# A hand-planned order for attention and the first MoE matmuls: table loads charged, engines held for attention, first k and v in other tiles

## The chip, the cores and the metric

One Trainium2 chip, one core. The time is the device time of one execution in microseconds. TensorE (PE) multiplies, VectorE (DVE), ScalarE (ACT) and GpSimd (POOL) work element by element, and all loads are issued by the queue of SyncE (SP).

## What is computed

Packed attention, then two MoE layers, in fp32:

```python
p_packed = sm_attn(p, k, v)                    # 4 batches, 8 heads, 576 positions, 64 wide; 32 packed queries
out = sm_attn(q, p_packed, p_packed)           # softmax attention, twice
x = out.transpose(0, 2, 1, 3).reshape(2304, 512)
h = x @ w_in                                   # 512 x 2048
x = (h * sigmoid(1.702 * h)) @ w_out           # 2048 x 512
pn = probs / (probs.sum(-1) + 1e-9)            # 4 experts
out = sum over e of pn[:, e] * (relu(x @ w1[e]) @ w2[e])
```

`w_in` and `w_out` come as 64 bit floats and have to be brought to fp32 on the chip.

## The kernel before

**Units.** Attention is cut in 8 units (`units`, 4 batches of 2 groups of 4 heads). `pack(u)` does the first attention of a unit: four times three transposes of k on TensorE, each with a copy on ScalarE (`kT`), two scores, two maxima on VectorE, two exps on ScalarE, transposes of the exps with copies (`kv`, L371), a product with v, the division, a last transpose and the split in a high and a low part. `unpack(u)` does the second: transposes of q with copies (`qT`), two scores, a 32 by 32 transpose on VectorE, maximum, exp, sum, division on POOL, back transpose and the split `a`. In the text p3 is the pack and u3 the unpack of unit 3.

**Matmuls.** All large products are done in three passes of fp32r parts, high times high, low times high, high times low. `packed_w` multiplies the packed values with a quarter of `w_in` (`win`) and evicts `pw` (`packed_w_out`: ScalarE casts, VectorE subtracts); `l1_first` multiplies `pw` with `a` and evicts by two gelus (`l1_out`); `l2_first` multiplies with `wout` and adds to the `y` tiles (`l2_out`). `l2_first` needs all four `wout` of its part. One block is 288 tokens, half of a batch; the second layer of a block runs one block behind the first.

**Conversions.** `fetch_w` loads a 512 KB piece of `w_in` or `w_out`; `convert` brings it to fp32 and splits it: six VectorE instructions, one of POOL, a cast on ScalarE and a subtraction on POOL. Eight pieces are converted in the head for the first quarter, and up to four more (`MORE`) once six unpacks (`UNITS_DONE`) are done.

**Order.** The head stands in `manual_schedule`: engines execute in the order in which the program is written. That order is made by the class `Order`. Each activity is a generator that yields, before every step, the engine, the planned time in us and the PSUM banks it takes; `Order.run` keeps a planned time for each engine (`at`) and always lets the step go that can start first, and at the same start the one with the lower rank. Evictions (`packed_w_out`, `l1_out`, `l2_out`) have rank 1, the two lanes of attention (`LANES`) 2 and 3, conversions 4, the lane of MoE matmuls 9. The lanes run p0 p2 u0 u2 p4 p6 u4 u6 and p1 p3 u1 u3 p5 p7 u5 u7. `load(FIRST)` issues the first loads: k and v of units 0 to 3 (`load_kv`), q of 0 and 1, and eight pieces of weights. When both lanes and the conversions are done, the main loop goes on outside of `manual_schedule`: the rest of the first MoE (`moe_step`), then the second one, whose order the scheduler of the framework makes.

**Memory.** One pool of 29 slots (`big`) holds loads, operands and intermediate tiles; a tile waits for the readers of the tile that had its slot. The three `y` tiles of pool `yp` take the result of the first MoE, 12 KB in each partition.

**Probabilities.** `norm_probs` loads `domain_probs` into `pr` and divides by the sums. It stands behind the head in the program, outside of `manual_schedule`, and ran at its start. `pr` is read by `l2_second` (L741, L743) alone.

The functions that the change touches, and what calls them:

Of the kernel before, what the change touches and what calls it, by code (L numbers as in the profile page):

```python
# [8 lines left out]
F32 = mybir.dt.float32  # L9
# [10 lines left out]

LANES = ("p0 p2 u0 u2 p4 p6 u4 u6", "p1 p3 u1 u3 p5 p7 u5 u7")
FIRST = "k0 k1 F F F F k2 k3 q0 q1 F F F F"
HOP = 0.25
UNITS_DONE = 6
MORE = 4


class Order:

    def __init__(self, banks):
        self.free = banks
        self.at = {}
        self.parts = []
        self.on = False

    def add(self, part, rank, at=0.0):

        if not self.on:  # L40
            return self.drain(part)
        self.parts.append([rank, at, next(part, None), part])

# [8 lines left out]
    def run(self, while_):  # L52
        self.on = True
        while while_():
            best = None
            for p in self.parts:
                rank, at, ask, part = p
                if callable(ask):
                    t = ask()
                    if t is None:  # L60
                        continue
                    p[1] = max(at, t)
                    p[2] = self.send(p, p[1])
                    best = p
                    start = None
                    break
                engine, us, banks = ask
                if banks > self.free:
                    continue
                start = max(at, self.at.get(engine, 0.0))  # L70
                if best is None or (start, rank) < best[0]:
                    best, start_ = ((start, rank), p), start
            if start is None:
                continue
            assert best is not None, [p[2] for p in self.parts]
            (start, _), p = best
            engine, us, banks = p[2]
            self.free -= banks
            self.at[engine] = start + us
            p[1] = start + us + HOP  # L80
            p[2] = self.send(p, p[1])
        self.on = False
# [15 lines left out]
def packed_attention_moe_kernel(  # L98
# [33 lines left out]
    big = ctx.enter_context(tc.tile_pool(name="big", bufs=29))  # L132
    small = ctx.enter_context(tc.tile_pool(name="small", bufs=2))
    hp = ctx.enter_context(tc.tile_pool(name="hp", bufs=4))
# [62 lines left out]
    def convert():  # L197
# [12 lines left out]
        f32 = man.bitcast(F32)  # L210
        yield "DVE", 0.83, 0

# [6 lines left out]
        )  # L219
        yield "DVE", 1.2, 0  # L220
        nc.vector.tensor_scalar(
# [25 lines left out]
    def load_kv(u):  # L247

        b, g = units[u]
        h0 = G * g  # L250
        sl = [slot([SP, 3 * R * D], F32, f"kv{u}{i}") for i in range(3)]
        m = 2 * R * D
        raws["k", u] = []
        for j in range(2):
            kk = sl[j][:, :m].rearrange("p (r h d) -> p r h d", r=R, h=2)
            for h in range(2):
                nc.sync.dma_start(out=kk[:, :, h, :], in_=k[b, h0 + 2 * j + h].rearrange("(p r) d -> p r d", r=R))
            raws["k", u].append(sl[j][:, :m])
        for j in range(2):
            vv = sl[j][:, m:].rearrange("p (r d) -> p r d", r=R)  # L260
            nc.sync.dma_start(out=vv, in_=v[b, h0 + j].rearrange("(p r) d -> p r d", r=R))
        vv = sl[2][:, :m].rearrange("p (h r d) -> p h r d", r=R, h=2)
        nc.sync.dma_start(out=vv, in_=v[b, h0 + 2:h0 + 4].rearrange("h (p r) d -> p h r d", r=R))
        arrives(("k", u), 1.18)
        raws["v", u] = [sl[0][:, m:], sl[1][:, m:], sl[2][:, :R * D], sl[2][:, R * D:m]]

# [12 lines left out]
    def transposed_scores(pair, dst, scores):  # L279

        for s in range(2):
            for j in range(2):
                yield "PE", 0.4, 1
                ps = psum("ps_t")
                for r in range(3):
                    nc.tensor.transpose(ps[:, r * SP:(r + 1) * SP], pair[j][3 * s + r], ident[:SP, :SP])
                t = yield "ACT", 0.4, 0
                nc.scalar.copy(out=dst[:, j, s * HS:(s + 1) * HS], in_=ps[:, :HS])
                order.free += 1
        for s in range(2):  # L290
            yield "PE", 0.6, 1
            yield from scores(s)
# [39 lines left out]
    def pack(u):  # L332
        b, g = units[u]
        kr, vr = raws.pop(("k", u)), raws.pop(("v", u))
        st = small.tile([128, 8], F32, tag="st", bufs=4, name=f"st{u}")
        kT = slot([128, 2, S], F32, f"kT{u}")
# [13 lines left out]
        for s in range(2):  # L350
            yield "ACT", 0.7, 0
            nc.scalar.activation(
                out=E[:, s * HS:(s + 1) * HS], in_=pss[s][:, :HS], func=AF.Exp,
                bias=st[:, 2:3], scale=scale, accum_out=st[:, 4 + s:5 + s],
            )
            order.free += 1
# [6 lines left out]
        for s in range(2):  # L363
            yield "PE", 0.45, 1
            ps = psum("ps_e")
# [6 lines left out]
            order.free += 1  # L372
        yield "PE", 1.0, 1
        ps = psum("ps_v")
# [40 lines left out]
    def unpack(u):  # L415
# [17 lines left out]
        nc.vector.tensor_sub(out=t, in0=t, in1=s2[:, 0, :].unsqueeze(2).to_broadcast([128, NB, NP]))  # L433
        yield "ACT", 0.7, 0
        nc.scalar.activation(out=t, in_=t, func=AF.Exp, scale=scale)
# [23 lines left out]
    def packed_w(a, bp):  # L459

        for g in range(UG):
# [11 lines left out]
            for b in (2 * bp, 2 * bp + 1):  # L473
                PW[a, b, g] = slot([128, 2, 512], F32R, f"pw{g}")
            order.add(packed_w_out(a, bp, g, pss), 1, clock())

# [16 lines left out]
    def l1_first(a, j, c):  # L493
# [16 lines left out]
        h = hid[a, j, c // 2][:, 2 * (c % 2):2 * (c % 2) + 2, :]  # L510
        order.add(l1_out(h, ps), 1, clock())

    def l1_out(h, ps):
        yield "ACT", 0.82, 0
        g32 = gp.tile([128, HS], F32, tag="g", name="g32")
# [6 lines left out]
    def l2_first(a, j, t):  # L522
# [21 lines left out]
        order.add(l2_out(a, j, t, ps), 1, clock())  # L544

# [210 lines left out]
    def norm_probs():  # L756
        nc.sync.dma_start(out=pr, in_=probs.rearrange("(t p) e -> p t e", p=128))
        nc.vector.reduce_sum(out=prs, in_=pr, axis=AX.X)
        nc.vector.tensor_scalar_add(prs, prs, 1e-9)
        nc.vector.reciprocal(out=prs, in_=prs)  # L760
        nc.vector.tensor_mul(out=pr, in0=pr, in1=prs.unsqueeze(2).to_broadcast([128, NT // 128, NE]))
# [112 lines left out]
    with tc.manual_schedule(engines=engines):  # L874
# [5 lines left out]
        all_p()  # L880
        load(FIRST)
        order.on = True
        lanes = [lane(x) for x in LANES] + [conversions(2 * CPP, MORE)]
        for i, x in enumerate(lanes):
            order.add(x, 2 + i)
        order.add(moe_lane(), 9)
        order.run(lambda: any(p[3] in lanes for p in order.parts))
        for p in list(order.parts):
            order.finish(p)
    norm_probs()  # L890
    b_parts = {i: b_operand(i) for i in range(NPAIR)}
# [63 lines left out]
```

## Time and profile before

| | us |
|---|---|
| median of 3 runs | 1252.76 |
| lowest, highest | 1251.65, 1253.18 |
| profiled execution | 1249.63 |
| its span, first to last instruction | 1247.4 |
| TensorE busy in the span | 1175.7 |
| VectorE busy | 899.5 |
| ScalarE busy | 523.6 |
| POOL busy | 483.0 |

Times in the rows below count from the first instruction. A row of the timeline is one instruction or several of the same kind in a row (x6): start, length, engine, line of the program, operation, what it writes and reads; in brackets the idle time of the engine ahead of it and what ended that. Matmuls overlap, so a busy TensorE is not one at its peak. An fp32 product counts as two instructions, a transpose or an fp32r product as one. The granted clock is 1.00 at 2.4 GHz and 0.50 at 1.2 GHz; a window shows its mean.

### The profile page before, as it was taken

The page shows a single profiled execution, that of the slowest core. Times are in us where ns is not written, and L with a number is a line of the kernel's source. Part 1 is how long each engine was busy: PE and PEld are TensorE (multiplying, and loading weights), DVE is VectorE, ACT ScalarE, POOL GpSimd, SP SyncE. Part 2 cuts the span into 40 slices and gives each one's busy share as a digit, 9 for nine tenths or more (in the row PEclk, how much of TensorE's full clock was granted, in tenths as well). Part 3 has the DMA queues.
Part 4 walks back from the last instruction along what each step waited for, and adds up shares of the span by engine and source line. Part 5 has one row for each costly group of instructions (what it writes and reads, how often), then busy time and mean ns, then how long its engine had stood idle before and what let it go on. Part 6 is the DMA issues. An engine that isn't in the chain of part 4 may idle for free. (4 is left out here: it accounts for less than half of the span.)

```text
span 1247.4 us, 18269 instructions
## 1 busy us (share of the span) xinstructions
PE 1175.7 (94%) x6912; PEld 1062.0 (85%) x6912; DVE 899.5 (72%) x1652; ACT 523.6 (42%) x1152; POOL 483.0 (39%) x409
## 2 busy tenths in 40 slices
PE   5778788999999989999999989999999999999998
PEld 4467577999999989999999969999999789999997
DVE  4873678786875856777777876777778767777775
ACT  3567655444434634433333444333333353333321
POOL 1320023221120345544444664444444744444430
PEclk8779989999999989999999989999999899999999
DMA  8623321121110012222222132222221332222201
GB/s 234 177 76 82 85 66 54 51 69 52 51 35 18 1 51 69 68 68 69 68 68 68 34 118 69 68 68 68 68 69 41 95 119 68 68 68 68 68 18 51
DMA packets 90392, 87.46 MB, mean 70 GB/s; under 512 B 43968, under 2 KB 71616, under 8 KB 90304
## 3 DMA queue, kind: packets, MB, share of 16 engines
q1 hardware_dynamic: 90304, 86.30, 23.1%
q8 instruction: 54, 0.88, 0.3%
q14 instruction: 34, 0.28, 0.1%
HBM read 81.56 MB, written 4.72 MB: 69 GB/s over the span
## 5 line engine op out<-in xcount | busy, mean ns | idle before, releaser
L732 PE MATMUL ps_o<-w,h 128*128 128x512 f32 x1728 | 449.9, 396 | 9.7 <-ACT h L688 5.5
L680 PE MATMUL ps_p<-b,w 128*128 128x384 f32 x2016 | 402.8, 339 | 0.6 <-DVE o L743 0.6
L680 PEld LDWEIGHTS ps_p<-b,w 128*128 128x128 f32 x2016 | 362.8, 189 | 24.6 <-DVE o L743 0.9
L732 PEld LDWEIGHTS ps_o<-w,h 128*128 128x128 f32 x1728 | 323.4, 189 | 63.6 <-DVE h L689 7.2
L154 POOL TENSOR_TENSOR w<-raw,w 128x512 fp32r<-128x512 f32 x192 | 236.4, 1250 | 172.3 <-ACT w L153 170.5
L528 PE MATMUL ps_acc<-h,wout 128*128 128x288 f32 x1536 | 232.9, 300 | 6.1 <-DVE h L520 6.1
L528 PEld LDWEIGHTS ps_acc<-h,wout 128*128 128x128 f32 x1536 | 215.1, 191 | 10.0 <-DVE h L520 7.3
L743 DVE SCALAR_TENSOR_TENSOR o<-ps_o,pr,o 128x512 f32<-128x512 f32 x270 | 200.0, 741 | 5.1 <-PE ps_o L732 5.1
L154 POOL TENSOR_TENSOR w<-s,w 128x512 fp32r<-128x512 f32 x96 | 132.6, 1381 | 170.4 <-ACT w L153 170.4
L500 PE MATMUL ps_h<-a,pw 128*128 128x288 f32 x768 | 129.9, 305 | 19.1 <-ACT a L446 12.6
L153 ACT CAST w<-raw 128x512 fp32r<-128x512 f32 x192 | 106.9, 562 | 72.4 <-POOL w L154 48.0
L500 PEld LDWEIGHTS ps_h<-a,pw 128*128 128x128 f32 x768 | 113.6, 195 | 22.9 <-ACT a L446 13.4
L520 DVE TENSOR_TENSOR h<-g,h 128x288 fp32r<-128x288 f32 x128 | 73.4, 575 | 63.0 <-ACT g L517 62.0
L649 DVE TENSOR_TENSOR s<-raw 128x256 f32<-128x256 f32 x48 | 48.5, 1010 | 86.1 <-DMA raw<-in_moe_w_dram 69.8
L516 ACT ACTIVATE h<-ps_h 128x288 fp32r<-128x288 f32 x128 | 53.1, 415 | 96.5 <-PE ps_h L500 95.9
L688 ACT ACTIVATE h<-uv 128x384 fp32r<-128x384 f32 x48 | 25.2, 526 | 162.5 <-DVE uv L720 162.5
L706 DVE TENSOR_TENSOR u<-ps_p,p 128x384 f32<-128x384 f32 x48 | 26.7, 556 | 70.4 <-ACT p L702 67.2
L153 ACT CAST w<-s 128x512 fp32r<-128x512 f32 x96 | 59.1, 615 | 41.9 <-DVE s L650 19.2
L217 POOL TENSOR_SCALAR cvt<-cvt 128x512 uint32<-128x512 uint32 x32 | 23.9, 747 | 127.0 <-DVE cvt L214 108.4
L688 ACT ACTIVATE h<-c 128x384 fp32r<-128x384 f32 x48 | 25.2, 525 | 92.5 <-DVE c L714 92.5
L688 ACT ACTIVATE h<-p 128x384 fp32r<-128x384 f32 x48 | 25.2, 526 | 82.4 <-DVE p L720 82.4
L553 DVE TENSOR_TENSOR y<-ps_acc,y 128x288 f32<-128x288 f32 (+2 forms) x120 | 44.7, 388 | 11.2 <-PE ps_acc L528 11.0
(102 smaller groups left out, 1169.5 us busy)
## 6 DMA issues: line engine op xcount, KB each, us to landing
raw<-in_moe_w_dram SPq DMA_DIRECT2D x96, 512.0 KB, 3.9
raw<-in_moe_w_in_dram SPq DMA_DIRECT2D x16, 512.0 KB, 4.1
raw<-in_moe_w_out_dram SPq DMA_DIRECT2D x16, 512.0 KB, 3.8
kv<-in_k_dram SPq DMA_DIRECT2D x32, 144.0 KB, 3.3
q<-in_q_dram SPq DMA_DIRECT2D x32, 144.0 KB, 2.9
out_dram<-o SPq DMA_DIRECT2D x18, 256.0 KB, 2.0
kv<-in_v_dram SPq DMA_DIRECT2D x16, 144.0 KB, 3.0
kv<-in_v_dram SPq DMA_DIRECT2D x8, 288.0 KB, 3.5
```

Source lines behind the costliest of these rows:

```text
L153: nc.scalar.copy(out=hi, in_=src)
L154: eng.tensor_sub(out=lo, in0=src, in1=hi.bitcast(F32))
L500: nc.tensor.matmul(out=ps[:, :HS], lhsT=PW[a, b, g][:, wp, c * 128:(c + 1) * 128], rhs=A[b * UG + g][:, xp, s * HS:(s + 1) * HS], start=(m ...
L516: nc.scalar.activation(out=h[:, 0, :], in_=ps[:, :HS], func=AF.Gelu_apprx_sigmoid)
L520: nc.vector.tensor_sub(out=h[:, 1, :], in0=g32, in1=h[:, 0, :].bitcast(F32))
L528: nc.tensor.matmul(out=ps[:, :HS], lhsT=W["out", a, c][:, wp, t * 128:(t + 1) * 128], rhs=hid[a, j, c // 2][:, 2 * (c % 2) + hq, :], start ...
L553: nc.vector.tensor_add(out=dst, in0=src, in1=dst)
L649: nc.vector.tensor_add(out=s1, in0=Am["A21"], in1=Am["A22"])
L680: nc.tensor.matmul(out=ps, lhsT=Wop[n, a, wp, kk], rhs=Bop[i, b, xp, kk], start=(m == 0), stop=(m == 5),)
L688: nc.scalar.activation(out=h[:, 0, :], in_=src, func=AF.Relu)
L732: nc.tensor.matmul(out=ps, lhsT=h[:, c, hq, o:o + 128], rhs=W2[n, c][:, wp, :], start=(c == 0 and m == 0), stop=(c == 1 and m == 2),)
L743: nc.vector.scalar_tensor_tensor(out=acc, in0=ps, scalar=pr[:, tok, e:e + 1], in1=acc, op0=ALU.mult, op1=ALU.add,)
```

## The change

- `Order.run` chooses the step with the smallest sum of planned start, `late` and a handicap. `late` is 1.28 (`TABLE`) for a ScalarE step that needs another function table than the one that the plan had last, and it also counts in the step's planned end. Lanes and evictions have handicap 0, the lane of MoE matmuls 0.3, conversions 0.6. At equal sums the one earlier in the list goes: lanes stand ahead of evictions. An engine may so be left idle in the plan for a step with a smaller handicap that can start a little later.
- The exps of `pack` and `unpack` name the table "exp", `l1_out` names "gelu".
- Planned times are longer: two of the three conversion steps on VectorE (0.83 to 0.9, 1.2 to 1.5), transposes (0.4 to 0.5), scores (0.6 to 0.9), the transposes of the exps (0.45 to 0.7) and the product with v (1.0 to 1.5) on TensorE.
- k and v of units 0, 1 and 2 (`EARLY`) are loaded into `y` tiles, not into nine slots of `big`.
- Pool `small` has 4 buffers, not 2.
- The load of `pr` is issued behind `load(FIRST)`, and `norm_probs` is the last thing in `manual_schedule`.

```diff
+EARLY = (0, 1, 2)
+TABLE = 1.28
-    def add(self, part, rank, at=0.0):
+    def add(self, part, handicap, at=0.0):
...
-            for p in self.parts:
-                rank, at, ask, part = p
-                if callable(ask):
-                    t = ask()
+            for p in list(self.parts):
+                while callable(p[2]):
+                    t = p[2]()
                     if t is None:
-                        continue
-                    p[1] = max(at, t)
+                        break
+                    p[1] = max(p[1], t)
                     p[2] = self.send(p, p[1])
-                    best = p
-                    start = None
-                    break
-                engine, us, banks = ask
+                if p not in self.parts or callable(p[2]):
+                    continue
+                engine, us, banks, table = (p[2] + (None,))[:4]
                 if banks > self.free:
                     continue
-                start = max(at, self.at.get(engine, 0.0))
-                if best is None or (start, rank) < best[0]:
-                    best, start_ = ((start, rank), p), start
+                start = max(p[1], self.at.get(engine, 0.0))
+                late = TABLE if table not in (None, self.table) else 0.0
+                if best is None or start + late + p[0] < best[0]:
+                    best = start + late + p[0], start + late + us, p
...
-    small = ctx.enter_context(tc.tile_pool(name="small", bufs=2))
+    small = ctx.enter_context(tc.tile_pool(name="small", bufs=4))
...
-        sl = [slot([SP, 3 * R * D], F32, f"kv{u}{i}") for i in range(3)]
+        n = R * D
+        if u in EARLY:
+            t = yp.tile([128, KD, 2 * TB], F32, tag="y", name=f"kv{u}").rearrange("p k t -> p (k t)")
+            sl = [t[:SP, x * 3 * n:(x + 1) * 3 * n] for x in range(2)] + [t[:SP, 6 * n:8 * n]]
+        else:
+            sl = [slot([SP, 3 * n], F32, f"kv{u}{i}") for i in range(3)]
...
-            yield "ACT", 0.7, 0
+            yield "ACT", 0.7, 0, "exp"
...
-        yield "ACT", 0.82, 0
+        yield "ACT", 0.82, 0, "gelu"
...
     def norm_probs():
-        nc.sync.dma_start(out=pr, in_=probs.rearrange("(t p) e -> p t e", p=128))
...
         load(FIRST)
+        nc.sync.dma_start(out=pr, in_=probs.rearrange("(t p) e -> p t e", p=128))
...
-        for i, x in enumerate(lanes):
-            order.add(x, 2 + i)
-        order.add(moe_lane(), 9)
+        for x in lanes[:-1]:
+            order.add(x, 0.0)
+        order.add(lanes[-1], 0.6)
+        order.add(moe_lane(), 0.3)
         order.run(lambda: any(p[3] in lanes for p in order.parts))
         for p in list(order.parts):
             order.finish(p)
-    norm_probs()
+        norm_probs()
```

## Rows read from the trace of the kernel before

**Rows 1.** Windows: stretch, its length, busy us (count) by engine, clock, DMA share, GB/s.

```profile
17.00:50.00 33.00, 25.87 (x293) 16.85 (x291) 27.96 (x61) 16.82 (x54) 14.91 (x19) 0.69 0.89 246
50.00:76.00 26.00, 12.43 (x56) 7.66 (x56) 24.91 (x40) 12.66 (x25) 7.37 (x7) 0.63 0.35 91
76.00:122.00 46.00, 43.86 (x390) 37.77 (x391) 19.91 (x46) 36.54 (x88) 3.52 (x6) 0.95 0.32 78
122.00:138.00 16.00, 10.89 (x154) 6.82 (x153) 5.92 (x15) 10.54 (x30) 0.74 (x3) 0.89 0.24 55
138.00:161.00 23.00, 12.56 (x89) 10.35 (x88) 18.33 (x33) 15.18 (x32) 3.92 (x5) 0.88 0.28 83
250.00:1247.00 997.00, 978.17 (x5322) 896.86 (x5321) 730.50 (x1325) 381.48 (x804) 427.07 (x341) 0.99 0.20 62
```

**Rows 2.** Waits of TensorE, whole span: who waited for whom, us, times, longest.

```profile
PE ps_s L297 <- DVE cvt L213: 8.1, 1, 8.1
PE ps_h L500 <- ACT pw L482: 5.0, 2, 4.6
PE ps_t L286 <- DMA kv<-in_k_dram: 2.6, 2, 1.6
```

**Rows 3.** Timeline of TensorE: start, length, what, and the wait ahead.

```profile
55.99 0.73 PE L297 MATMUL ps_s<-qT,pT 128*64 128x288 f32 x2 [1.63 <-ACT qT L288]
...
74.63 1.77 PE L500 MATMUL ps_h<-a,pw 128*128 128x288 f32 x5 [2.81 <-ACT a L446]
...
81.87 1.02 PE L528 MATMUL ps_acc<-h,wout 128*128 128x288 f32 x6
...
160.74 1.57 PE L500 MATMUL ps_h<-a,pw 128*128 128x288 f32 x5 [8.62 <-ACT a L446]
```

**Rows 4.** Timeline of ScalarE, in 50:76.

```profile
64.75 0.62 ACT L235 CAST wout<-cvt 128x512 fp32r<-128x512 f32 x1 [5.99 <-DVE cvt L231]
```

**Rows 5.** Timeline of SP and VectorE, start; then a load's size and landing time.

```profile
1.24 0.57 SPq L757 DMA_DIRECT2D pr<-in_moe_domain_probs_dram  x1
1.85 3.97 SPq L257 DMA_DIRECT2D kv<-in_k_dram  x4
...
5.18 0.22 DVE L758 TENSOR_REDUCE prs<-pr 128x18 f32<-128x72 f32 x1
...
pr<-in_moe_domain_probs_dram SPq DMA_DIRECT2D x1, 36.0 KB, 3.6
```

**Rows 6.** Timeline of VectorE and POOL, in 58:74.

```profile
58.08 2.85 DVE L486 TENSOR_TENSOR pw<-ps_w,pw 64x512 fp32r<-64x512 f32 x4
...
64.59 0.48 DVE L425 STREAM_TRANSPOSE t<-ps_s 128x288 f32<-128x288 f32 x1
...
70.10 1.16 POOL L441 TENSOR_TENSOR t<-t,s 128x576 f32<-128x576 f32 x1 [0.54 <-DMA kv<-in_k_dram]
...
73.05 0.77 DVE L443 STREAM_TRANSPOSE t<-t 128x576 f32<-128x576 f32 x1
```

**Rows 7.** Conversions: window of tile cvt (VectorE, ScalarE, POOL); last step on POOL.

```profile
17.00:76.00 59.00, 32.25 (x48) 4.94 (x8) 15.36 (x16) 0.66 0.65 178
...
73.86 1.27 POOL L237 TENSOR_TENSOR wout<-cvt,wout 128x512 fp32r<-128x512 f32 x1 [2.60 <-ACT wout L235]
```

**Rows 8.** Timeline of TensorE and ScalarE: p6 from 121.9, then q of u5 and u6.

```profile
121.94 0.49 PE L368 MATMUL ps_e<-ident,kT 128*96 128x128 f32 x3
...
121.93 1.28 ACT L516 ACT_TABLE_LOAD   x1
123.22 0.41 ACT L516 ACTIVATE h<-ps_h 128x288 fp32r<-128x288 f32 x1
...
124.44 0.52 ACT L371 COPY kv<-ps_e 96x384 f32<-96x384 f32 x1
...
142.14 0.41 PE L286 MATMUL ps_t<-ident,q 96*128 96x96 f32 x3
...
145.95 0.39 ACT L288 COPY qT<-ps_t 128x288 f32<-128x288 f32 x1
```

More of the change, by code (lines that the diff above doesn't have):

```diff
@@ L36, in __init__ @@
         self.on = False
-    def add(self, part, rank, at=0.0):
+        self.table = None
+    def add(self, part, handicap, at=0.0):
         if not self.on:
             return self.drain(part)
-        self.parts.append([rank, at, next(part, None), part])
+        self.parts.append([handicap, at, next(part, None), part])
     def drain(self, part):
@@ L55, in run @@
             best = None
-            for p in self.parts:
-                rank, at, ask, part = p
-                if callable(ask):
-                    t = ask()
+            for p in list(self.parts):
+                while callable(p[2]):
+                    t = p[2]()
                     if t is None:
-                        continue
-                    p[1] = max(at, t)
+                        break
+                    p[1] = max(p[1], t)
                     p[2] = self.send(p, p[1])
-                    best = p
-                    start = None
-                    break
-                engine, us, banks = ask
+                if p not in self.parts or callable(p[2]):
+                    continue
+                engine, us, banks, table = (p[2] + (None,))[:4]
                 if banks > self.free:
                     continue
-                start = max(at, self.at.get(engine, 0.0))
-                if best is None or (start, rank) < best[0]:
-                    best, start_ = ((start, rank), p), start
-            if start is None:
-                continue
+                start = max(p[1], self.at.get(engine, 0.0))
+                late = TABLE if table not in (None, self.table) else 0.0
+                if best is None or start + late + p[0] < best[0]:
+                    best = start + late + p[0], start + late + us, p
             assert best is not None, [p[2] for p in self.parts]
-            (start, _), p = best
-            engine, us, banks = p[2]
+            _, end, p = best
+            engine, us, banks, table = (p[2] + (None,))[:4]
             self.free -= banks
-            self.at[engine] = start + us
-            p[1] = start + us + HOP
+            self.at[engine] = end
+            self.table = table or self.table
+            p[1] = end + HOP
             p[2] = self.send(p, p[1])
@@ L210, in convert @@
         f32 = man.bitcast(F32)
-        yield "DVE", 0.83, 0
+        yield "DVE", 0.9, 0
         nc.vector.tensor_scalar(out=ex, in0=hi, scalar1=0x7FF00000, scalar2=None, op0=ALU.bitwise_and)
@@ L219, in convert @@
         )
-        yield "DVE", 1.2, 0
+        yield "DVE", 1.5, 0
         nc.vector.tensor_scalar(
@@ L264, in load_kv @@
         arrives(("k", u), 1.18)
-        raws["v", u] = [sl[0][:, m:], sl[1][:, m:], sl[2][:, :R * D], sl[2][:, R * D:m]]
+        raws["v", u] = [sl[0][:, m:], sl[1][:, m:], sl[2][:, :n], sl[2][:, n:m]]
     def load_q(u):
@@ L282, in transposed_scores @@
             for j in range(2):
-                yield "PE", 0.4, 1
+                yield "PE", 0.5, 1
                 ps = psum("ps_t")
@@ L290, in transposed_scores @@
         for s in range(2):
-            yield "PE", 0.6, 1
+            yield "PE", 0.9, 1
             yield from scores(s)
@@ L334, in pack @@
         kr, vr = raws.pop(("k", u)), raws.pop(("v", u))
-        st = small.tile([128, 8], F32, tag="st", bufs=4, name=f"st{u}")
+        st = small.tile([128, 8], F32, tag="st", name=f"st{u}")
         kT = slot([128, 2, S], F32, f"kT{u}")
@@ L363, in pack @@
         for s in range(2):
-            yield "PE", 0.45, 1
+            yield "PE", 0.7, 1
             ps = psum("ps_e")
@@ L372, in pack @@
             order.free += 1
-        yield "PE", 1.0, 1
+        yield "PE", 1.5, 1
         ps = psum("ps_v")
@@ L433, in unpack @@
         nc.vector.tensor_sub(out=t, in0=t, in1=s2[:, 0, :].unsqueeze(2).to_broadcast([128, NB, NP]))
-        yield "ACT", 0.7, 0
+        yield "ACT", 0.7, 0, "exp"
         nc.scalar.activation(out=t, in_=t, func=AF.Exp, scale=scale)
@@ L474, in packed_w @@
                 PW[a, b, g] = slot([128, 2, 512], F32R, f"pw{g}")
-            order.add(packed_w_out(a, bp, g, pss), 1, clock())
+            order.add(packed_w_out(a, bp, g, pss), 0.0, clock())
     def packed_w_out(a, bp, g, pss):
@@ L510, in l1_first @@
         h = hid[a, j, c // 2][:, 2 * (c % 2):2 * (c % 2) + 2, :]
-        order.add(l1_out(h, ps), 1, clock())
+        order.add(l1_out(h, ps), 0.0, clock())
     def l1_out(h, ps):
-        yield "ACT", 0.82, 0
+        yield "ACT", 0.82, 0, "gelu"
         g32 = gp.tile([128, HS], F32, tag="g", name="g32")
@@ L543, in l2_first @@
                     ACC[i] = yp.tile([128, KD, 2 * TB], F32, tag="y", name=f"y{i}")
-        order.add(l2_out(a, j, t, ps), 1, clock())
+        order.add(l2_out(a, j, t, ps), 0.0, clock())
     def l2_out(a, j, t, ps):
```

## Prediction

> **What bounds the kernel now.** I read the windows by stage first [rows 1]. From 250 us to the end TensorE is busy 978 of 997 us: that is matmul work which the change doesn't touch. Before it, in the head (attention, with the first MoE work in its gaps), TensorE idles 13.6 of 26 us in 50:76 and 15.5 of 39 in 122:161, but only 2.1 of 46 in 76:122. TensorE is full afterwards, so a microsecond of matmul work that moves forward into a hole comes off the end; that is all the change can be worth.
>
> The waits of TensorE and its timeline name the holes. *Hole A* is 8.1 us up to the scores of u2 [rows 2] and 2.8 us up to 74.63, where the first `l1_first` gets `a` of u1; the second layer begins at 81.87 [rows 3]. ScalarE's queue shows one reason: the cast of a `wout` stood 6.0 us at its head, waiting for a VectorE conversion [rows 4], and in that order the `qT` copies that u2's scores need stood behind it. VectorE is what ended last: busy 24.9 of 26 us there and 28.0 of 33 in the stretch before [rows 1]. *Hole B*: the matmuls of batches 0 and 1 run out before attention delivers p7 and u5; the longest piece is the 8.6 us up to 160.74, for `a` of u5 [rows 3]. A *third hole*, 4.6 us for `pw` [rows 2], lies in the main loop.
>
> **The change part by part.** The sum is made against the profiled execution (1249.63 us, span 1247.4); the median of the runs shown is 1252.76, 3.13 more, and that is added at the end.
>
> *Probabilities.* The load of `pr` goes from ahead of the first k to behind FIRST; it takes 0.57 us of the SP queue, and the first k, now issued at 1.85, can go at about 1.28 [rows 5]. The start waits for loads, so I take 0.6. Bounds: 0, and the 3.6 us that this load needs to land [rows 5], if it holds up the others that long. Four small VectorE instructions (the first takes 0.22 [rows 5], so 0.9 together) move to the end of the head, after which `pr` is not read before the second MoE. Beside VectorE's other work they cost nothing; without cover 0.9.
>
> *First k and v in the y tiles, small pool of 4.* Nothing is computed otherwise; nine `big` slots are free sooner and loads that wait for slots can go earlier. TensorE waits for k loads only at the start, 2.6 us in two pieces [rows 2], when slots are not short yet. So 0; bounds 0 and 2.6. The y tiles are wanted at 81.87, when the packs of u0 to u2 are long done: no new wait.
>
> *Order in hole A.* The path is u1. Its second score ended at 56.72 [rows 3]; VectorE transposed it at 64.59, 7.9 us late, after `pw` evictions (2.85 for the second four) and steps of u0 [rows 6]. Its back transpose could go when POOL ended at 71.26 and went at 73.05, 1.8 late, behind conversion steps [rows 6]. Together 9.7. In the new order a lane step goes before an eviction that could start at the same time, and a conversion step starts only if no lane step is due within 0.6. Steps of 1.4 us that already run still have to end, and u0's own stay: I take half, 4.8. The new planned times, 3.76 us a conversion for 3.39, are nearer to the 32.25 us that VectorE took for eight, 4.03 each [rows 7], so casts should be queued less early. l1 then goes on at 69.8 rather than 74.63, and the second layer at 77.1 rather than 81.87. The next thing late would be the last `wout`, done at 75.13 [rows 7]: it just fits. Gain 4.8; far bound the two waits, 10.9; near bound a loss, the first rival.
>
> *Order in hole B.* After the exps of a pack ScalarE now changes to gelu, runs two of them, and only then copies what TensorE transposed. In p6 the first transposes end at 122.43 and the copy starts at 124.44, 2.0 late, with the table load and the gelus between [rows 8]; p4 and p5 show the same pattern. With 1.28 charged to the gelu the copy is due first. Lane 1 ends last and has one such pack, p5: 2.0. Then u5 and u6: q transposed by 142.55 were copied at 145.95, 3.4 late, behind gelu and `pw` casts [rows 8]; lanes now go first, I take 3.0. The granted clock in 138:161 is 0.88 [rows 1], part of it at the lower level after the wait; at full clock the 12.56 us of matmuls would be 1.5 shorter; I take 1.0. Sum 6.0; bounds 0 and 15.5, all idle of 122:161.
>
> *The charge against its price.* From the table load at 121.93 to the gelu is 1.29 us [rows 8], so 1.28 is right here. The Trainium skill (ScalarE: Activation LUTs, What ACT_TABLE_LOAD costs) gives 2.66 us for a switch, the load and a drain of 1.38 behind it. By that the plan would stay 1.38 short at every switch and the gain would come out as in the third rival. The rows show no such drain.
>
> *Waits that the change adds.* The 0.3 of the MoE lane makes the plan hold TensorE before a matmul chunk if a lane step is due so soon. Between 76 and 162 there are 76 lane steps on TensorE (4 packs of 10, 6 unpacks of 6), one each 1.1 us, so a chunk meets one with a chance of 0.27 and then waits 0.15 on the mean; 66 chunks (22 pairs of one l1 and two halves of an l2) give 2.7 us. Queued behind are matmuls, whose readers have slack. Part of it falls into time that is idle anyway: I take 1.3; bounds 0 and 2.7. The 0.6 of the conversions belongs to the first rival.
>
> *Main loop.* Its third hole depends on when conversions of the next part of `w_in` and `w_out` end against TensorE; both move with the head. Taken as unchanged; bounds 4.6 either way.
>
> Sum: 0.6 + 4.8 + 6.0 - 1.3 = 10.1 us. An execution like the profiled one then takes 1239.5, the median 1242.7.
>
> **The rivals.**
> *VectorE waits for attention and conversions come late (slower).* In 17:76 VectorE idles only 6.1 us [rows 1]. The plan may add up to 0.6 before each of 32 lane steps (4 packs of 5, 2 unpacks of 6), 19.2 at most, and the second layer needs all four `wout`. It decides from 6.7 us of added idle on: 75.13 + 6.7 is the 81.87 of now. At half the ceiling the second layer is 2.9 late, at all of it 12.5. For it: VectorE is the bound there. Against it: the plan waits only where a conversion is ready and a lane step near. With 4 us late, hole B moved along with it, and 0.6 gained at the start: 1256.2.
>
> *The gaps only change place (no change).* Attention comes earlier, but the MoE work that it passes comes later, and TensorE is 95% busy in 76:122 [rows 1]. For it: the plan now overstates TensorE at full clock (0.5 for three transposes that took 0.41 [rows 8]), so its order is off the other way. The 10.1 is lost again: 1252.8.
>
> *ScalarE still runs late against the plan (half the gain).* The exp is charged too, so gelus pass it, 0.7 us a pair by [rows 8], and copies of evictions with them; hole B then gives 1.5, not 6. 0.6 + 4.8 + 1.5 - 1.3 = 5.6: 1247.2.
>
> *Both holes close.* 10.9 of A and all but 3 of B's 15.5: 0.6 + 10.9 + 12.5 - 1.3 = 22.7: 1230.1.
>
> **How the numbers follow.** Forecast 0.42, half the gain 0.13, both holes 0.09: faster. No change 0.14. Late conversions 0.18 and a longer third hole 0.04: slower. So faster by over 0.2% (2.5 us, about what a measurement of this kernel can tell from no change) 0.64, within it 0.14, slower 0.22. The likeliest is 1242.7. The range takes in most of the closed holes on one side and the late conversions up to about 5 us on the other: 1229 to 1258.
>
> **What would show it.** Right: TensorE over 16 us busy in 50:76, l1 past its first step before 71, the second layer before 79; the `kv` copies on ScalarE directly behind the exps, ahead of any table load; the wait for `a` near 160 under 5 us. Wrong: VectorE idle over 12 us in 17:76 and a last `wout` after 80 (first rival); the same idle sum of TensorE in 50:161, spread over more waits (second); copies on time but p7 and u5 no earlier (third). The prediction fails if VectorE isn't what ends last in hole A, or if the order of the main loop, which nothing in the head pins, comes out otherwise.

## The result and the profile after

The changed kernel takes 1241.88 us (median of 4 runs, 1239.13 to 1243.16), the kernel before beside it 1252.2: ratio 0.9914, 95% interval 0.9896 to 0.9932. On a second chip, with 6 runs, it was 0.9899 (0.9872 to 0.9925). The forecast was 1242.7. The profiled execution took 1241.1 us, span 1239.2, where the one of before had 1249.63 and 1247.4. Lines stand lower in the changed file, those of the conversions by one (L235 is L236), most others by seven: L446 of before is L453, L482 is L489, L500 is L507, L516 is L523, L528 is L535.

The windows of the changed kernel (stretch, its length, busy us and count of PE, PEld, DVE, ACT and POOL, clock, DMA share, GB/s), to be read against [rows 1]:

```profile
17.00:50.00 33.00, 24.67 (x280) 17.06 (x281) 27.16 (x56) 17.58 (x55) 15.14 (x19) 0.63 0.90 234
50.00:76.00 26.00, 16.93 (x79) 9.91 (x79) 23.52 (x40) 11.78 (x26) 5.59 (x6) 0.76 0.37 93
76.00:122.00 46.00, 42.83 (x425) 35.97 (x426) 21.80 (x50) 33.68 (x91) 6.28 (x10) 0.92 0.36 88
122.00:138.00 16.00, 14.43 (x133) 11.88 (x134) 9.14 (x19) 12.65 (x31) 1.98 (x3) 0.89 0.20 41
138.00:161.00 23.00, 16.00 (x98) 13.14 (x98) 18.02 (x33) 12.68 (x27) 2.98 (x3) 0.78 0.28 90
```

TensorE gained 4.5 us of busy time in 50:76 (12.43 to 16.93) and 7.0 in 122:161 (23.45 to 30.43); it lost 1.2 in 17:50 and 1.0 in 76:122. These are the two holes that the prediction named, and about the sizes it gave them. Busy isn't quite work, though: from 150 to 158 us the changed kernel is busy for 4.8 us at a granted clock of 0.50, and the kernel before for only 0.3 us at that level in the whole of 138:161. Six matmuls took 1.79 us there that take 1.06 at the full clock (last section), so some 2 us of the 7.0, an estimate from these rows, are the same work at the lower clock. The timeline of TensorE shows what is left of them (compare [rows 3]):

```profile
66.31 1.52 PE L304 MATMUL ps_s<-qT,pT 128*64 128x288 f32 x4 [5.96 <-ACT qT L295]
...
71.79 0.80 PE L507 MATMUL ps_h<-a,pw 128*128 128x288 f32 x4 [1.45 <-ACT a L453]
...
84.02 2.48 PE L304 MATMUL ps_s<-kT,pT 128*64 128x288 f32 x8 [2.65 <-ACT kT L295]
...
86.88 1.79 PE L535 MATMUL ps_acc<-h,wout 128*128 128x288 f32 x6
...
153.24 1.57 PE L507 MATMUL ps_h<-a,pw 128*128 128x288 f32 x5 [7.00 <-ACT a L453]
...
205.51 0.61 PE L507 MATMUL ps_h<-a,pw 128*128 128x288 f32 x1 [6.04 <-ACT pw L489]
```

In hole A the scores of u2 wait 6.0 us instead of 8.1 and the second step of `l1_first` starts at 71.79 instead of 74.63. What is left of the wait stands in ScalarE's queue again, behind a cast of `a` that waited 4.8 us for VectorE, and an exp:

```profile
63.87 0.67 ACT L453 CAST a<-t 128x576 fp32r<-128x576 f32 x1 [4.75 <-DVE t L450]
...
65.29 0.68 ACT L442 ACTIVATE t<-t 128x576 f32<-128x576 f32 x1 [0.75 <-DVE t L440]
65.88 1.28 ACT L295 COPY qT<-ps_t 128x288 f32<-128x288 f32 x4
```

But the second layer starts at 86.88: *later* than the 81.87 of before. In hole B `a` of u5 is awaited for 7.0 us up to 153.24; before it was 8.6 up to 160.74, so everything there happens 7.5 us earlier. The third hole, in the main loop, is 6.0 us; it was 4.6 [rows 2].

The late second layer is a late conversion in the plan, which lets `l2_first` go only when all four `wout` of its part are planned. The window of tile `cvt` in 17:76 (VectorE, ScalarE, POOL) has 43 VectorE steps where before had 48 [rows 7]:

```profile
17.00:76.00 59.00, 28.29 (x43) 4.36 (x7) 13.89 (x14) 0.69 0.66 172
```

The missing five are of the last `wout`; from the timelines of VectorE, ScalarE and POOL:

```profile
75.66 0.43 DVE L215 TENSOR_SCALAR cvt<-cvt 128x512 uint32<-128x512 uint32 x1
...
83.58 0.42 DVE L222 TENSOR_SCALAR cvt<-raw 128x512 uint32<-128x512 uint32 x1
...
86.48 1.52 DVE L232 SCALAR_TENSOR_TENSOR cvt<-cvt 128x512 f32<-128x512 f32 x1
...
88.11 0.62 ACT L236 CAST wout<-cvt 128x512 fp32r<-128x512 f32 x1 [3.25 <-DVE cvt L232]
...
88.81 1.28 POOL L238 TENSOR_TENSOR wout<-cvt,wout 128x512 fp32r<-128x512 f32 x1 [1.35 <-ACT wout L236]
```

Behind its second step VectorE left it for 7.5 us (76.09 to 83.58) and worked for u2, u3 and the first gelus. It ends at 90.1; before it ended at 75.13 [rows 7]. TensorE doesn't wait for it at 86.88: the six matmuls there read the first two `wout`, and the program has them that late.

The start is 0.6 us earlier, as predicted: the first k is issued at 1.24 and no longer at 1.85 [rows 5], the load of `pr` goes at 35.44, and the sums run at 187.33 in the middle of other work (SP and VectorE):

```profile
1.24 2.71 SPq L264 DMA_DIRECT2D kv<-in_k_dram  x4
...
35.44 0.81 SPq L888 DMA_DIRECT2D pr<-in_moe_domain_probs_dram  x1
...
187.33 0.21 DVE L764 TENSOR_REDUCE prs<-pr 128x18 f32<-128x72 f32 x1
```

Where the 8.2 us of span came from, by the start of the same matmul in both traces: 0.4 earlier at the first `packed_w`, 5.0 *later* at the second layer, 4.4 earlier at `packed_w` of batches 2 and 3 (137.40 to 132.96), 8.9 earlier at `packed_w` of the second part (200.68 to 191.75), 7.5 behind the third hole, 6.5 at the first product that is weighted by `pr`, in the second MoE (482.05 to 475.57), 8.2 at the end. So the gain arises between 88 and 192 us, in attention, in spite of hole A.

### The profile page after: what moved, and what is told of

Same layout as the page of the kernel before. It is cut to its first block, busy times and chain, and to the rows that moved or that the text cites. A ratio compares the mean times of both kernels' runs of the same rounds, so it can differ in the third digit from the quotient of the medians.

```text
span 1239.2 us, 18237 instructions
## 1 busy us (share of the span) xinstructions
PE 1176.0 (95%) x6912; PEld 1060.9 (86%) x6912; DVE 891.6 (72%) x1652; ACT 519.4 (42%) x1146; POOL 483.0 (39%) x409
## 5 line engine op out<-in xcount | busy, mean ns | idle before, releaser
L535 PE MATMUL ps_acc<-h,wout 128*128 128x288 f32 x1536 | 236.7, 302 | 4.8 <-DVE h L527 4.8
L535 PEld LDWEIGHTS ps_acc<-h,wout 128*128 128x128 f32 x1536 | 218.3, 193 | 8.9 <-DVE h L527 5.5
L507 PE MATMUL ps_h<-a,pw 128*128 128x288 f32 x768 | 128.6, 303 | 14.9 <-ACT a L453 8.4
L507 PEld LDWEIGHTS ps_h<-a,pw 128*128 128x128 f32 x768 | 112.5, 193 | 18.3 <-ACT a L453 8.9
L523 ACT ACTIVATE h<-ps_h 128x288 fp32r<-128x288 f32 x128 | 52.9, 414 | 100.8 <-PE ps_h L507 100.2
L218 POOL TENSOR_SCALAR cvt<-cvt 128x512 uint32<-128x512 uint32 x32 | 24.0, 751 | 125.0 <-DVE cvt L215 110.0
```

The source lines that it names most:

```text
L507: nc.tensor.matmul(out=ps[:, :HS], lhsT=PW[a, b, g][:, wp, c * 128:(c + 1) * 128], rhs=A[b * UG + g][:, xp, s * HS:(s + 1) * HS], start=(m ...
L523: nc.scalar.activation(out=h[:, 0, :], in_=ps[:, :HS], func=AF.Gelu_apprx_sigmoid)
L535: nc.tensor.matmul(out=ps[:, :HS], lhsT=W["out", a, c][:, wp, t * 128:(t + 1) * 128], rhs=hid[a, j, c // 2][:, 2 * (c % 2) + hq, :], start ...
```

## The experiments

Two readings were open. *By parts*: the gain comes from what the prediction named, the charge for table loads, lanes ahead of evictions, the handicap of conversions. *By luck*: any shuffle of a hand-made order moves the time by several us, and this one fell well. Each run stands against the kernel before on the same chip. Beside the ratio the table gives three readings of each trace: the start of the second layer (first L535), the start of the last cast of `a` in the head (L453), and TensorE's busy time in 50:184.

| kernel | ratio (95% interval) | second layer | last `a` | TensorE busy 50:184 |
|---|---|---|---|---|
| before | 1 | 81.9 | 182.5 | 102.5 |
| evictions ahead of lanes | 0.9995 (0.9981 to 1.0010) | 79.1 | 185.9 | 103.5 |
| before, lanes ahead of evictions | 0.9977 (0.9963 to 0.9991) | 82.0 | 181.0 | 108.6 |
| MoE handicap 0 | 0.9972 (0.9960 to 0.9985) | 86.6 | 178.6 | 110.0 |
| old rule, rest of the change | 0.9959 (0.9946 to 0.9973) | 83.6 | 179.8 | 109.7 |
| HOP 0.22 | 0.9935 (0.9913 to 0.9956) | 87.9 | 179.9 | 108.7 |
| HOP 0.30 | 0.9930 (0.9912 to 0.9949) | 93.0 | 175.8 | 107.9 |
| changed kernel | 0.9914 (0.9896 to 0.9932) | 86.9 | 172.7 | 113.2 |
| k and v in the big pool | 0.9904 (0.9883 to 0.9925) | 84.8 | 174.3 | 111.7 |
| changed kernel, second chip | 0.9899 (0.9872 to 0.9925) | 86.5 | 171.0 | 113.1 |
| conversions' handicap 0.3 | 0.9896 (0.9879 to 0.9914) | 81.7 | 172.5 | 112.4 |
| no charge for table loads | 0.9896 (0.9881 to 0.9911) | 89.8 | 164.4 | 115.0 |
| weights of next part earlier | 0.9869 (0.9845 to 0.9893) | 84.8 | 168.3 | 113.1 |
| the same, no charge | 0.9855 (0.9830 to 0.9880) | 88.5 | 161.7 | 114.4 |

**The changed kernel once more.**

> The changed kernel itself once more, beside the same runs of before as the next three, so that each of them stands against it on one chip. Expected ratio to before 0.991; a spread of its median by over 2 us from 0.991 would say that differences of 2 us between the variants are not to be read.

1238.84 us against 1249.94 (medians; the ratio goes by all runs and lies nearer to that of the means). The middle of the ratio moves by 0.0015, 1.9 us, from one chip to the other.

**Two shuffles.** `HOP` is the planned time between the end of one step of a chain and its next; one run has 0.22, the other 0.30:

```
-HOP = 0.25
+HOP = 0.22
```

> The changed kernel with the planned step from one engine to the next (HOP) at 0.22 instead of 0.25; a control without meaning of its own, which only shuffles the order of the head. Theory (each part works by what it does): time within 2 us of the changed kernel, ratio 0.989 to 0.992. Rival (any shuffle of the order moves the time by several us, so that the effects of handicaps and ties are in part luck): 0.987 or less, or 0.994 or more.

> The changed kernel with HOP at 0.30 instead of 0.25; the second control. Theory: within 2 us of the changed kernel, ratio 0.989 to 0.992. Rival (luck of the order): 0.987 or less, or 0.994 or more.

0.9935 and 0.9930, between the two readings: by the ratios 2 to 4.5 us slower than the changed kernel (this and the other differences below are taken against both of its ratios), mostly beyond the 2 us of the first and just short of the bound of the second. The intervals overlap those of the changed kernel, which was not run on this chip, so the loss isn't clear of noise. What can be said is that a shuffle may be worth up to 4.5 us, and that an effect of 4 us or less of one edit to the rule says nothing about that edit's mechanism. Nor is `HOP` wholly without meaning: it is a planned time like the others, and 0.25 may be the better one. Both runs still beat the kernel before by 8 us, so these two shuffles leave the larger part. The kernel before was not shuffled with its own rule; whether its order was an unlucky one stays open. Even the third hole is dealt out by the shuffle: with HOP at 0.22 TensorE waits 2.9 us for `pw` there and no longer 6.0 (busy 63.0 of 66 us in 184:250, 60.0 in the changed kernel), so that less of this kernel's 8 us comes from the head.

**Conversions' handicap.**

```
-        order.add(lanes[-1], 0.6)
+        order.add(lanes[-1], 0.3)
```

> The changed kernel with the handicap of the conversions at 0.3 instead of 0.6. Theory (the handicap makes the wout conversions late and so costs hole A what the prediction hoped to gain there): the last wout cast ends several us before the 88.8 us of the changed kernel, the second layer begins before 84, and the time is 1 to 4 us lower (1238 to 1241) if the attention lanes keep their place. Rival (VectorE has no room: what conversions gain the lanes lose): a of u1 and the transposes of p4/p5 come 1 us or more later, and the time is the same or up to 4 us longer. A third view (any shift of the order moves the time by some us in either direction): neither milestone moves in that pattern.

The last `wout` was cast at 83.26 instead of 88.11 and the second layer began at 81.66, as the theory had it. p4 gave way to it (its first `kv` copy 102.62 for 92.89), the end of attention didn't: the last `a` came at 172.5 for 172.7. The time didn't follow: 0.9896 beside 0.9899 and 0.9914. The late conversion is real and costs nothing that these runs can tell. That is the rival's picture in p4, though not in `a` of u1 (cast at 70.77 for 71.07). The column of the second layer says it over all runs: the earliest start (79.1) belongs to a kernel that gained nothing, the second latest (89.8) to one of the best.

**The charge for table loads.**

```
-TABLE = 1.28
+TABLE = 0.0
```

> The changed kernel with the charge for a table load at 0 instead of 1.28. Theory (the charge brings the copies of the transposed exps ahead of the gelus, and with it the packs p4 to p7): table loads after the first rise from 11 towards the 17 of before, hole B (idle of TensorE in 122:161) grows from 8.6 us by 2 to 4, and the time is 2 to 4 us longer (1244 to 1246). Rival (the gain is the lanes standing ahead of evictions, the charge does little): time within 1 us of the changed kernel. A loss of the whole gain (1250 and more) would say that the charge is all of it.

The loads rose from 11 to 17 behind the first, as expected, but the time didn't: 0.9896. Hole B didn't grow, it nearly closed. The windows of this kernel:

```profile
76.00:122.00 46.00, 38.01 (x409) 28.48 (x409) 20.61 (x50) 33.29 (x86) 5.40 (x9) 0.89 0.37 91
122.00:138.00 16.00, 16.00 (x116) 13.16 (x115) 9.15 (x17) 11.02 (x25) 1.76 (x3) 1.00 0.31 86
138.00:161.00 23.00, 21.72 (x148) 17.89 (x148) 18.77 (x34) 21.23 (x44) 3.52 (x4) 1.00 0.15 47
```

TensorE is busy for 37.7 of the 39 us (30.4 with the charge). ScalarE is busy 8.6 us longer in 138:161, five table loads of 1.28 in it where the changed kernel has two, and had that room. The last `a` comes 6 to 8 us earlier, probably because exps no longer let gelus pass; no run tests that. In time it is worth nothing that can be told from the changed kernel. Most of the idle has moved: in 76:122 TensorE is busy 38.0 us for 42.8, and of the 7.3 us gained in 122:161 only 1.8 are left over 50:184 (115.0 for 113.2). What can be said is that the charge brings no gain here.

**The handicap of the MoE lane.**

```
-        order.add(moe_lane(), 0.3)
+        order.add(moe_lane(), 0.0)
```

> The changed kernel with the handicap of the MoE lane at 0 instead of 0.3. Prediction's step (the handicap only makes TensorE wait, 1.3 us): 1.3 us faster, 1240.6, with the lanes' milestones in place. Rival (the handicap is what lets lane steps on TensorE start on time): transposes and scores of p4 to p7 come later, a of u5 comes after 155, and the time is 2 us or more longer (1244 and more).

0.9972, 7 to 9 us slower than the changed kernel, well beyond the shuffles; the rival's direction and more than its size. Up to 101 us the two orders run alike. Then MoE chunks go ahead of lane steps: the first transposes of p7 start at 117.11 instead of 114.90, its last scores at 124.59 instead of 121.88, its first exp at 128.84 instead of 125.34. At 128 the MoE work on batches 0 and 1 is used up in both kernels, so the chunks that went ahead are missing there. TensorE's timeline with handicap 0:

```profile
126.62 1.77 PE L535 MATMUL ps_acc<-h,wout 128*128 128x288 f32 x12
...
129.49 0.53 PE L375 MATMUL ps_e<-ident,kT 128*96 128x128 f32 x3 [1.10 <-ACT kT L359]
130.54 0.82 PE L375 MATMUL ps_e<-ident,kT 128*96 128x128 f32 x3 [0.52 <-ACT kT L359]
...
134.63 0.31 PE L384 MATMUL ps_v<-kv 96*32 96x64 f32 x1 [2.48 <-ACT kv L378]
```

In the changed kernel that `ps_v` is over by 131, and `a` of u5 lets TensorE go on at 153.24, here at 158.91. The handicap costs nothing because the work that it holds back runs dry in any case; lane steps that it lets through lead to the next work.

**Evictions ahead of lanes.**

```
-            order.add(packed_w_out(a, bp, g, pss), 0.0, clock())
+            order.add(packed_w_out(a, bp, g, pss), -0.01, clock())
...
-        order.add(l1_out(h, ps), 0.0, clock())
+        order.add(l1_out(h, ps), -0.01, clock())
...
-        order.add(l2_out(a, j, t, ps), 0.0, clock())
+        order.add(l2_out(a, j, t, ps), -0.01, clock())
```

> The changed kernel, with evictions ahead of lane steps at equal sums (handicap -0.01 for the three evictions) instead of behind them. Prediction's step (lanes ahead of evictions bring the q copies of u5 and u6 and u1's transpose forward, 3 us in hole B): a of u5 returns from 152.5 towards 156 and the time is 3 us longer (1245). Rival (ties are rare, the handicaps of MoE and conversions decide): within 1 us.

The whole gain is gone: 0.9995, 10 to 12 us slower than the changed kernel, three to four times what was expected. Little of it is lost where it was expected: hole B ends at 153.22 as in the changed kernel, with TensorE busy 28.0 us in 122:161 for 30.4. The largest loss of busy time is at the last units, 18.7 us in 161:184 for 23.0, with another wait behind it. VectorE, ScalarE and TensorE of this kernel (the gelu stands for five pairs):

```profile
167.06 0.76 DVE L440 TENSOR_TENSOR t<-t,s 128x576 f32<-128x576 f32 x1
...
168.38 0.41 ACT L523 ACTIVATE h<-ps_h 128x288 fp32r<-128x288 f32 x1 [0.39 <-PE ps_h L507]
...
180.04 1.28 ACT L442 ACT_TABLE_LOAD   x1
181.33 0.68 ACT L442 ACTIVATE t<-t 128x576 f32<-128x576 f32 x1
...
185.88 0.67 ACT L453 CAST a<-t 128x576 fp32r<-128x576 f32 x1 [3.87 <-DVE t L450]
...
186.61 1.87 PE L507 MATMUL ps_h<-a,pw 128*128 128x288 f32 x5 [6.88 <-ACT a L453]
```

The input of the last exp is ready at 167.82 and the exp's table load starts at 180.04, 12.2 us later. In the plan the exp has to start 1.28 sooner than a gelu to be chosen, and a new gelu comes with every `l1_first`, so it waits until the MoE work is used up. Then TensorE waits 6.9 us for `a`. In the changed kernel the same exp was ready at 165.17 and its load started at 167.04, 1.9 later:

```profile
167.04 1.28 ACT L442 ACT_TABLE_LOAD   x1
168.33 0.69 ACT L442 ACTIVATE t<-t 128x576 f32<-128x576 f32 x1
```

So the charge can starve the step it is put on, and which side wins hangs on a tie of 0.01. This run shows that pair of edits together; it doesn't price the tie without the charge.

**Lanes ahead of evictions, alone.** In the kernel before, the rank of all three evictions:

```
-            order.add(packed_w_out(a, bp, g, pss), 1, clock())
+            order.add(packed_w_out(a, bp, g, pss), 3.5, clock())
```

> The kernel before with one edit: evictions have rank 3.5 instead of 1, so that at the same planned start both lanes of attention go ahead of them (and of the conversions); all else as before. Theory (lanes ahead of evictions are the part that carries the gain, as putting evictions ahead in the changed kernel lost all of it): the last split a of the head is cast before 177 instead of 182.5 and the ratio to before is 0.992 to 0.996. Rival (the order of ties only works together with the handicaps and the new planned times): ratio 0.998 to 1.002.

0.9977, about 3 us, less than the theory had and within what a shuffle may do. The last `a` came at 181.0, not before 177. Hole A closed in part (the scores of u2 waited 2.8 us instead of 8.1), hole B fell from 8.6 to 5.6 us. The theory that this edit by itself carries the gain falls.

**The old rule with the rest of the change.** The rule chooses by start and rank, with the ranks of before, and has neither handicaps nor a charge. The line of the choice:

```
...
-            if best is None or start + late + p[0] < best[0]:
+            if best is None or (start, p[0]) < best[0]:
...
```

> The changed kernel with the old rule of choice (earliest planned start, at a tie the rank: evictions, lanes, conversions, MoE), no handicaps and no charge for table loads; the new planned times, the move of the probabilities and the place of the first k and v stay. Theory (the gain is the rule): the time goes back to 1248 to 1252, a of u5 to about 160, and a of u1 to about 75. Rival (the gain is the planned times or the tiles): 1241 to 1245.

0.9959, 1243.78 us: in the range that the rival gave, although that range was set for a chip on which the kernel before took 1252, not 1249. As a share it is between the two: without the new rule there is a gain of 5 us. Of what is left in this kernel the start gives 0.6 and the tiles nothing (next run), so the new planned times give up to 4.5, which is about what a shuffle may give. The last `a` comes at 179.8, and u2's scores wait 9.4 us: hole A is as open as before. The rule adds 5.6 to 7.5 us to that.

**The place of the first k and v.**

```
-EARLY = (0, 1, 2)
+EARLY = ()
```

> The changed kernel with the first k and v in the big pool as before (no early units in the y tiles). Prediction's step (worth nothing): within 1 us of the changed kernel. Rival (slots of the big pool are short in the first 76 us and the change frees nine): conversions or loads begin later in 17:76, DMA share there falls below 0.90, and the time is 2 to 4 us longer.

0.9904: no difference, and a DMA share of 0.88 for 0.90 in 17:50. As predicted, this part is worth nothing that can be told. The pool `small` of 4 was not taken back in any run.

**The third hole.** In the list of MoE matmuls, `packed_w` of the next part one second-layer step earlier:

```
             moe.append((l1_first, (a, j, c), None))
+            if c == 1 and j == NB1 - 1 and a + 1 < n_pass1:
+                moe.append((packed_w, (a + 1, 0), None))
             if i > 0:
                 moe.append((l2_first, blocks1[i - 1] + (c,), ("first",) + blocks1[i - 1] + (c,)))
...
-            if c == 1 and j % 4 == 3:
+            if c == 1 and j % 4 == 3 and j < NB1 - 1:
```

> The changed kernel with one edit in the list of MoE matmuls: the weights of the next part (packed_w of part 1, 2, 3, first half) stand one second-layer step earlier, ahead of the step whose end triggers a conversion of w_out. Theory (the third hole, 6.0 us before 205.51, is the casts of pw queued on ScalarE behind a cast of wout that waits for VectorE): the hole falls to under 2 us and the time falls by 3 to 6 us. Rival (TensorE runs dry because the first layer needs pw whatever the queue; VectorE's subtraction of pw is as late): the wait moves to another reader and the time stays within 1.5 us.

0.9869, 3.7 us below the changed kernel on the same chip by the middle of the ratios; the intervals overlap a little. The head is planned as in the changed kernel (113.1 us busy in 50:184 in both; its last `a` at 168.3 for 171.0 and 172.7 shows how far that reading moves from one execution to the next), and the trace shows the mechanism itself. ScalarE in the changed kernel, then in this one:

```profile
203.75 0.62 ACT L236 CAST wout<-cvt 128x512 fp32r<-128x512 f32 x1 [3.84 <-DVE cvt L232]
204.28 4.08 ACT L489 CAST pw<-ps_w 64x512 fp32r<-64x512 f32 x7
```

```profile
193.49 0.62 ACT L236 CAST wout<-cvt 128x512 fp32r<-128x512 f32 x1 [0.27 <-DVE cvt L232]
194.01 1.18 ACT L489 CAST pw<-ps_w 64x512 fp32r<-64x512 f32 x2
```

In the changed kernel the casts of `pw` stand behind a cast of `wout` that waits 3.8 us for VectorE, although `packed_w` ended by 194.7. With the order changed they start at 194.01, and TensorE waits 0.4 us for `pw` and no longer 6.0. Its window for 184:250:

```profile
184.00:250.00 66.00, 63.49 (x445) 60.68 (x445) 51.62 (x105) 32.74 (x79) 17.03 (x15) 1.00 0.18 56
```

TensorE is busy 63.5 of 66 us, for 60.0 in the changed kernel, and the clock stays at 1.00.

**Both edits together.**

No charge, and the list of MoE matmuls of the last run:

```
-TABLE = 1.28
+TABLE = 0.0
...
+            if c == 1 and j == NB1 - 1 and a + 1 < n_pass1:
+                moe.append((packed_w, (a + 1, 0), None))
...
```

> The changed kernel without the charge for table loads and with the weights of the next part one step earlier, the two edits that each ran at or below the changed kernel (ratios 0.9896 and 0.9869 against 0.9899). Theory (the third hole and the lanes are separate places): the gain of the earlier weights, 3 to 5 us, comes on top of what the missing charge gives: ratio 0.984 to 0.987. Rival (the third hole was filled by what the other left): 0.988 or more.

0.9855, 1231.27 us for 1248.19: the lowest ratio of this study, 17 to 18 us below the kernel before. The interval lies below that of the missing charge alone (0.9881 to 0.9911), so the earlier weights bring some 5 us here as well; it overlaps that of the earlier weights alone (0.9845 to 0.9893), so what the missing charge adds to them isn't shown. The trace has the marks of both: TensorE is busy 37.7 us in 122:161 and 62.9 in 184:250.

## Why the prediction was right, and where its steps failed

The number was right: 1241.88 for 1242.7, inside the range, with the sign forecast at 0.64. The mechanism (order in two holes, work moved into them) is the one the traces show. The steps are right in part.

- *Start, 0.6*: right, to the row (1.24 for 1.85).
- *Tiles, 0*: right, by the run without them.
- *Hole A, 4.8*: the busy time came (16.93 where "over 16" was to show it, l1 running at 69.97, though past its first step only at 71.79 where 71 was the bound), the second layer didn't (86.88, "before 79" was to show it). The first rival's mechanism took place in this hole, half of its signs too: the last `wout` at 90.1, but VectorE idle 8.3 us in 17:76, not 12. What failed is the link from the second layer to the end. The prediction took the start of that layer for the worth of the hole and priced the rival by it (2.9 us late at half the ceiling). It is 5.0 late and the kernel is faster; with an earlier one (81.66) the time is the same. The 4.5 us went to attention and first-layer work: 14 matmuls of `l1_first` by 76 us instead of 6, and the transposes of p4 and p5 from 80.21 on instead of 86.24. At 122 us the second layer is 24 matmuls behind before (96 for 120), and no wait of TensorE comes from them.
- *Hole B, 6.0*: the size was about right, its terms were not. TensorE goes on 7.5 us earlier behind the hole (153.24 for 160.74), and its idle time in 122:161 is 8.6 us for 15.5, though some 2 of these 6.9 are work at the lower clock. The sign set for it, a wait near 160 under 5 us, wasn't reached (7.0). The 2.0 for the charge: the copies stand directly behind the exps in p4 and p7 as predicted (92.89 and 93.96 ahead of the load at 95.45; 127.66 and 128.81 ahead of 129.31), but not in p5 and p6, where one goes at 108.30 and three stand behind the load at 108.79 (from 110.68); p5 is the pack that the 2.0 was taken from. And without the charge the hole closes further. The third term, 1.0 for the clock, was misread: in the kernel before the clock fell to 0.50 at about 156, with TensorE idle, so that of the 12.56 us in 138:161 only 0.3 ran at that level and there was next to nothing to give back. The 3.0 for lanes ahead: alone it gives about 3 in all, and turned round in the changed kernel, with the charge, it costs 10 to 12, the largest part of it where the exp starves.
- *Waits of the MoE lane, 1.3 lost*: wrong in sign. It is worth 7 to 9 us of what the changed kernel has. The step multiplied chances of waiting and left out what the waits are for: a lane step that goes on time opens the next batch's work, and the chunk held back has nothing behind it that is missed.
- *The charge against its price*: the Trainium skill (ScalarE: Activation LUTs, What ACT_TABLE_LOAD costs) was weighed with 2.66 us for a switch, which would have left the plan short. No run here shows the drain: in the changed kernel the load at 167.04 is followed by the exp at 168.33, 1.29 later. The price was right and the charge brought no gain even so.
- *Planned times*: no term in the sum; with the old rule they and the start give 5 us, of which a shuffle might give most. That part stays open.
- *Third hole, unchanged*: 1.5 us longer, inside its bound.

The terms don't add up either: the runs that take one part out lose 10 to 12, 7 to 9 and 0 us, against 11 to 13 in all. What ties the runs together, roughly, is when attention ends: the last `a` at 178 to 186 goes with ratios from 0.9935 up, at 171 to 176 with 0.989 to 0.993. Earlier still buys little: without the charge it comes at 164.4, and TensorE is nearly full in 122:161 but has 4.8 us less in 76:122. That the end of attention is the cause, and not a companion of the time, is argued from the waits for `a`; no run changed it alone, and the reading itself moves by some 4 us between executions of one order.

That the total came out within 1 us was luck in part: errors of opposite sign cancelled (the MoE lane, the charge, the second layer), and a shuffle of the same rule may be worth up to 4.5 us.

## What to carry to other kernels

In an order planned by hand, find the work that opens more work (here attention for the next batches) and let work that will run dry in any case give way to it; when a dependent stage started, or how often a function table was loaded, said little about the end here. Before crediting an edit to such an order, shuffle the order with a number that means nothing and read no effect smaller than what that does. Look in the main loop for an eviction queued behind one that waits for another engine: moving one line of a list there cut a wait of 6.0 us to 0.4, and gave 3.7 us by the middle of the ratios.

## What the runs showed of the hardware

The same VectorE instruction on the same shape took up to three times as long where POOL worked beside it. Rows of the changed kernel, first POOL, then VectorE twice:

```profile
67.50 1.16 POOL L448 TENSOR_TENSOR t<-t,s 128x576 f32<-128x576 f32 x1 [5.17 <-DVE s L446]
...
67.58 1.35 DVE L215 TENSOR_SCALAR cvt<-cvt 128x512 uint32<-128x512 uint32 x1
...
75.66 0.43 DVE L215 TENSOR_SCALAR cvt<-cvt 128x512 uint32<-128x512 uint32 x1
```

1.35 us beside a POOL product, 0.43 with POOL idle (its next step, L218, starts at 76.24). The Trainium skill (SBUF — State Buffer, Who interferes with whom) says that VectorE's two-port modes and GpSimd take turns on a shared pair of ports and that the later of the two waits for the whole of the other's instruction. These rows agree: L215 begins 0.08 behind the product and ends 0.27 behind its end (68.93, 68.66). No run here took the product away, so that the cause is argued. The planner gives each step one time, so no planned time fits both; that is one limit of any such plan.

TensorE's clock fell behind the wait of hole B, in both kernels. In the changed kernel TensorE stopped at 146.2; the granted clock was 1.00 in 144:146, 0.60 in 148:150 and 0.50 from 150 to 158, the last 4.7 us of it with TensorE at work again. In the kernel before TensorE stopped at 152.1; the clock was 1.00 in 150:154 and 0.50 from 156 to 165, with TensorE at work again from 160.74. So a 7 us wait costs more than 7 us: six `l2_first` matmuls took 1.79 us there (154.99) and 1.06 at the full clock (141.55). In the kernel without the charge, where TensorE idles 1.3 us in all of 122:161, the clock stayed at 1.00 there. The mean clock of a window doesn't say this: 138:161 has 0.78 in the changed kernel and 0.88 before, because the work at the lower level falls inside it in one and behind its end in the other.
